# Talking-heads attention with a squared-ReLU feed-forward: PSUM as three two-bank tiles and two single banks, merged copies, and the first batch's feed-forward in three token groups

## The chip, the cores and the metric

The kernel runs on one core of one Trainium2 chip. The metric is the device time of one execution in microseconds, and a kernel's time is the median of its runs. A ratio is the mean time of one kernel's fast runs over that of the other kernel's fast runs of the same rounds on the same chip, with a 95% interval, so it is not quite the ratio of the medians that are quoted beside it. A difference of over 2% counts as faster or slower.

Engines are named as in the profile: PE multiplies matrices, DVE and ACT copy and compute, POOL computes `d` and `h` here (360 times 641 ns and 128 times 931 ns in the kernel before), PEld is PE's weight load.

## The reference

Eight batches of attention with 12 heads, 448 tokens and 64 dimensions per head. Scores are mixed across heads before and after the softmax, and the result goes through a two-layer feed-forward.

```python
scores = scale * np.matmul(q, k.transpose(0, 1, 3, 2))
scores = np.einsum('bhij,hg->bgij', scores, w_pre)      # mix over heads
scores = scores - np.max(scores, axis=-1, keepdims=True)
attn = np.exp(scores)
attn = attn / (np.sum(attn, axis=-1, keepdims=True) + 1e-09)
attn = np.einsum('bhij,hg->bgij', attn, w_post)         # mix over heads again
attn_out = np.matmul(attn, v)
# ... [cut: heads put side by side: x is 3584 x 768]
h = np.maximum(x @ w_in, 0.0)                            # w_in is 768 x 2048
out = h * h @ w_out                                      # w_out is 2048 x 768
```

## The kernel before

The work on one batch is cut into 45 tiles of up to 10 query rows (all 12 heads of them). The kernel goes through the tiles two at a time; such a pair is called a **step** here, and a batch has 22.5 steps. In a step PE makes:

- `s_ps`: scores of a head pair for a coming block; ACT or DVE copies them to the buffer S, and a DMA gathers S into tiles G with heads and rows side by side;
- `m_ps`: the first mixing of two tiles; ACT takes the exponential, POOL normalises into `d`;
- `at_ps`: the second mixing of the two tiles mixed two steps earlier; DVE casts the result into `at`.

Between these there are four kinds of larger work: `tr_ps` (transposes of the next batch's k and q, six units per batch), `ot_ps` (attention times v, two units after each of three parts of a batch), and the feed-forward of the batch before, `h_ps` (first layer, 16 units) and `o_ps` (second layer, 7 tiles in two halves each). The feed-forward is a filler: it is dealt out evenly over the steps.

```python
psp = ctx.enter_context(tc.tile_pool(name="psp", bufs=8, space=bass.MemoryType.PSUM))
def bank(name, dtype=F32):                     # all eight banks are one pool
    return psp.tile([P, 512 if dtype == F32 else 1024], dtype, name=name, tag="ps")

def score_burst(b, blk, pairs):
    # ... [cut]
    for p in pairs:
        for hh in range(2):
            # ... [cut]
            ps = bank("s_ps")
            nc.tensor.matmul(ps[:, 0:S], ...)
            got.append((2 * p + hh, ps))
    for h, ps in got:                          # one copy per head, one bank each
        if h % 2 == 0 or (b == 0 and h in (3, 9)):
            nc.scalar.copy(out=sb[:, h, :], in_=ps[:, 0:S])
        else:
            nc.vector.tensor_copy(out=sb[:, h, :], in_=ps[:, 0:S])

def unmix(pair):
    us = [bank("at_ps") for _ in range(2)]     # two banks, two casts
    # ... [cut]

def fill(ns):                                  # the filler, with a debt
    owed[0] += ns
    while filler and owed[0] > 0:
        w, f = filler.pop(0)
        f()
        owed[0] -= w
    # ... [cut]
# ... [cut: most of the loop over the steps]
    fill(share)
    for w, f in now:                           # transposes and ot_ps units of this step
        f()
        owed[0] -= w                           # their time is taken from the filler
```

The softmax here doesn't subtract the row's maximum and nothing guards it: scores larger than these inputs give would overflow.

## Time and profile before

| | before |
|---|---|
| median of 3 runs | 639.2 us (638.43 to 642.54) |
| span of the profiled run, mean granted clock | 637.8 us, 0.942 |
| busy: PE, DVE, ACT, POOL | 580.7, 414.9, 403.5, 405.7 us |

The page cuts the span into 40 slices of 15.9 us. Of the kernel before, these are the rows of PE's busy share and of its granted clock, both in tenths (9 is 90% or more):

```profile
PE   4558678699999999999999999999999999999897
PEclk9675686799999999999999999999999999999899
```

The first eight slices, up to some 125 us, are a different regime: PE is busy 0.4 to 0.8 of the time and its clock, from the second slice on, is at 0.5 to 0.8. (The 9 of the first slice is not a clock that was granted: the trace's clock records begin with the first change, at 14.1 us here, and the row counts the time before it as full. Sixteen `tr_ps` matmuls took 0.96 us at 5.5 us, and 0.56 us at 38.7 us, where the recorded clock is full.) After that PE is over 90% busy at full clock (1.00 from 124 to 580 us) until the last batch's feed-forward. The stretches view (start and end in us, length, busy time and instruction count of PE, PEld, DVE, ACT and POOL, then granted clock, share of the DMA engines and GB/s) of the kernel before:

```profile
60.00:100.00 40.00, 28.27 (x344) 11.85 (x338) 27.16 (x73) 26.66 (x84) 23.65 (x36) 0.71 0.72 126
...
191.60:226.00 34.40, 33.62 (x420) 17.28 (x421) 26.28 (x65) 27.32 (x79) 31.39 (x44) 1.00 0.68 110
297.70:327.30 29.60, 29.41 (x421) 16.79 (x414) 24.05 (x60) 18.73 (x60) 13.93 (x23) 1.00 0.68 140
```

In the first row nothing is saturated. In the second (a batch's first-layer half) PE has 33.62 of 34.40 us and POOL 31.39; in the third (a second-layer half) PE has 29.41 of 29.60.

The waits view (who waited for whom; us in total, times, the longest) of the kernel before, 0 to 119 us, shows that score copies wait for the gathers that still read the buffer they are to overwrite:

```profile
ACT S L296 <- DMA G<-S: 24.0, 5, 7.5
...
DVE S L298 <- DMA G<-S: 13.7, 4, 4.9
```

The groups of copies that the change merges, from the page of the kernel before (line, engine, operation, output<-input, shapes, count | busy us, mean ns of one | idle time just before, what ended most of it):

```profile
L351 DVE CAST at<-at_ps 112x480 bf16<-112x480 f32 x352 | 221.3, 669 | 41.7 <-PE at_ps L344 41.1
...
L296 ACT CAST S<-s_ps 128x448 bf16<-128x448 f32 x200 | 105.9, 550 | 55.7 <-PE s_ps L291 27.4
...
L298 DVE CAST S<-s_ps 128x448 bf16<-128x448 f32 x184 | 110.6, 607 | 16.3 <-DMA G<-S 13.7
```

PE's own waits of the kernel before, from the start of step 48 to that of step 179 (181.8 to 580.3 us, almost six batches):

```profile
PE o_ps L254 <- POOL h L232: 2.1, 3, 0.9
PE s_ps L291 <- ACT e_sb L319: 1.0, 5, 0.2
PE at_ps L344 <- ACT xt L192: 0.9, 2, 0.5
...
```

And a piece of PE's timeline of the kernel before (start us, duration us, what; the count is of single matmuls). Three transpose units and two `ot_ps` units, each with a bank of its own, follow each other without a gap:

```profile
178.51 0.58 PE L162 MATMUL tr_ps<-ident,kst 112*64 112x112 bf16 x16
178.93 0.56 PE L162 MATMUL tr_ps<-ident,qst 112*64 112x112 bf16 x16
179.32 0.56 PE L162 MATMUL tr_ps<-ident,kst 112*64 112x112 bf16 x16
179.71 1.61 PE L181 MATMUL ot_ps<-at,v 112*64 112x138 bf16 x48
181.25 0.39 PE L344 MATMUL at_ps<-post,d 60*128 60x60 bf16 x16
```

### The profile page before, as it was taken

To read this page: it belongs to the slowest core of one execution; us is meant where nothing else is said; L and a number is where in the kernel's file an instruction comes from. 1 tells how busy PE (TensorE), PEld (TensorE's weight loads), DVE (VectorE), ACT (ScalarE), POOL (GpSimd) and SP (SyncE) were. 2 spreads that over 40 slices of the span, in tenths; PEclk is the share of its full clock that TensorE was granted. 3 is DMA by queue.
4 is the path that set the end of the run, shared out by engine and by line. 5 is a ranking of instruction groups with operands and counts; after the bars stand their busy time and mean duration, and the time that the engine had idled before them with its cause. 6 is when DMAs were issued, how large, how long until landed. Compare 5 with 4: busy or idle time off the path is not lost.

```text
span 637.8 us, 19148 instructions
## 1 busy us (share of the span) xinstructions
PE 580.7 (91%) x7338; PEld 313.8 (49%) x7338; DVE 414.9 (65%) x1050; ACT 403.5 (63%) x1196; POOL 405.7 (64%) x583
## 2 busy tenths in 40 slices
PE   4558678699999999999999999999999999999897
PEld 3125234345555456455555455545555555555454
DVE  3366666566777767777787677776787677755101
ACT  3656567477467865887578756886587757862330
POOL 6343558699448963888468943897387746873350
PEclk9675686799999999999999999999999999999899
DMA  9884869997655785578646885488543655432002
GB/s 135 141 170 85 153 108 197 197 187 111 139 113 89 127 150 121 92 110 136 140 103 106 135 157 104 87 135 135 126 94 74 110 128 103 81 61 64 25 7 81
DMA packets 90880, 73.61 MB, mean 115 GB/s; under 512 B 6308, under 2 KB 87716, under 8 KB 90788
## 3 DMA queue, kind: packets, MB, share of 16 engines
q1 hardware_dynamic: 51842, 49.57, 34.6%
q0 software_dynamic: 38816, 22.81, 27.8%
q8 instruction: 57, 0.93, 0.6%
q14 instruction: 35, 0.29, 0.1%
q10 hardware_dynamic: 130, 0.01, 0.0%
HBM read 45.63 MB, written 11.01 MB: 89 GB/s over the span
## 4 chain that ended last, share of the span: by engine, by line
PE 67%; POOL 11%; ACT 8%; DMA 5%; DVE 4%; SPq 2%; issue 2%; ACTq 0%; POOLq 0%; DVEq 0%
PE o_ps L254 23%; PE h_ps L227 18%; PE m_ps L316 9%; PE at_ps L344 6%; PE ot_ps L181 5%; POOL d L323 5%; DMA G<-S 4%; POOL h L232 4%; PE s_ps L291 4%; ACT xt L192 3%; ACT e_sb L319 3%; PE tr_ps L162 2%; SPq L310 2%; DVE at L351 2%; ACT S L296 2%
## 5 line engine op out<-in xcount | busy, mean ns | idle before, releaser
L323 POOL TENSOR_SCALAR d<-e_sb,rc 128x448 bf16<-128x448 f32 x360 | 226.7, 641 | 178.0 <-DVE rc L321 175.3
L351 DVE CAST at<-at_ps 112x480 bf16<-112x480 f32 x352 | 221.3, 669 | 41.7 <-PE at_ps L344 41.1
L319 ACT ACTIVATE e_sb<-m_ps 128x448 f32<-128x448 f32 x360 | 195.4, 556 | 59.2 <-PE m_ps L316 51.0
L227 PE MATMUL h_ps<-xt,w 128*128 128x448 bf16 x768 | 167.0, 357 | 0.2 <-ACT e_sb L319 0.2
L254 PE MATMUL o_ps<-w,h 128*128 128x384 bf16 (+1 forms) x1024 | 162.4, 327 | 2.1 <-POOL h L232 2.1
L296 ACT CAST S<-s_ps 128x448 bf16<-128x448 f32 x200 | 105.9, 550 | 55.7 <-PE s_ps L291 27.4
L232 POOL TENSOR_TENSOR h<-hr 128x448 bf16<-128x448 f32 x128 | 118.4, 931 | 26.9 <-ACT hr L231 26.5
L298 DVE CAST S<-s_ps 128x448 bf16<-128x448 f32 x184 | 110.6, 607 | 16.3 <-DMA G<-S 13.7
L316 PE MATMUL m_ps<-G,pre 120*128 120x448 bf16 x360 | 108.0, 374 | 14.4 <-DMA G<-S 6.2
L254 PEld LDWEIGHTS <-h 128*128 128x128 bf16 (+1 forms) x1024 | 85.4, 100 | 71.2 <-issue 16.8
L321 DVE RECIPROCAL rc<-sm 128x1 f32<-128x1 f32 x360 | 55.8, 159 | 99.1 <-ACT e_sb L319 96.2
L227 PEld LDWEIGHTS <-w 128*128 128x128 bf16 x768 | 71.4, 98 | 76.8 <-issue 17.0
L231 ACT ACTIVATE hr<-h_ps 128x448 f32<-128x448 f32 x128 | 70.4, 550 | 44.1 <-PE h_ps L227 33.7
L344 PEld LDWEIGHTS <-d 60*128 60x128 bf16 x2880 | 54.7, 96 | 75.4 <-issue 54.6
L344 PE MATMUL at_ps<-post,d 60*128 60x60 bf16 x2880 | 76.6, 192 | 8.7 <-ACT S L296 6.0
L291 PE MATMUL s_ps<-kT,qT 64*128 64x448 bf16 x384 | 78.2, 370 | 3.1 <-ACT e_sb L319 1.3
L319 ACT ACTIVATION_READ_ACCUMULATOR e_sb<-m_ps 128x1 f32 x360 | 77.9, 216 | 0.0
L192 ACT ACTIVATE xt<-ot_ps,bvec 128x160 bf16<-128x160 f32 (+3 forms) x144 | 42.8, 392 | 43.5 <-PE ot_ps L181 30.8
L316 PEld LDWEIGHTS <-pre 120*128 120x128 bf16 x360 | 29.6, 99 | 54.3 <-issue 25.1
L181 PE MATMUL ot_ps<-at,v 112*64 112x160 bf16 (+4 forms) x1152 | 46.6, 242 | 9.6 <-ACT S L296 5.9
L261 DVE COPY osb<-o_ps 128x384 f32<-128x384 f32 x48 | 26.4, 551 | 39.0 <-PE o_ps L254 37.9
L181 PEld LDWEIGHTS <-v 112*64 112x64 bf16 x1152 | 43.1, 118 | 14.8 <-issue 12.0
(35 smaller groups left out, 189.7 us busy)
## 6 DMA issues: line engine op xcount, KB each, us to landing
G<-S SPq DMA_DIRECT2D x352, 105.0 KB
kst<-in_k_dram POOLq DMA_DIRECT2D x24, 224.0 KB, 5.9
qst<-in_q_dram POOLq DMA_DIRECT2D x24, 224.0 KB, 5.5
v<-in_v_dram POOLq DMA_DIRECT2D x24, 224.0 KB, 6.6
w<-in_moe_w_in_dram POOLq DMA_DIRECT2D x8, 384.0 KB, 6.5
w<-in_moe_w_out_dram POOLq DMA_DIRECT2D x8, 384.0 KB, 9.6
out_dram<-osb SPq DMA_DIRECT2D x8, 336.0 KB
out_dram<-osb SPq DMA_DIRECT2D x8, 288.0 KB
```

Of the source, the lines that this page charges most:

```text
L181: nc.tensor.matmul(ps[64 * hh:64 * hh + 64, TW * y + c0:TW * y + 2 + n], lhsT=vs[b][0:PR, g, r, :], rhs=at[0:PR, r, g, c0:2 + n], start=(y ...
L227: nc.tensor.matmul(ps[:, 0:S], lhsT=w1[ft // 4][:, c2, ft % 4 * 128:ft % 4 * 128 + 128], rhs=xts[b][:, c2, :], start=(c2 == 0), stop=(c2 = ...
L232: nc.gpsimd.tensor_tensor(out=h2[:, :], in0=hr[:, :], in1=hr[:, :], op=ALU.mult)
L254: nc.tensor.matmul(dst, lhsT=h2ts[(b, ft)][:, mt * 128:mt * 128 + ROWS[mt]], rhs=w2[ft // 4][:, ft % 4, n2 * 384:(n2 + 1) * 384], start=(f ...
L291: nc.tensor.matmul(ps[:, 0:S], lhsT=qTs[b][rs, p, BLK_START[blk]:BLK_START[blk] + P], rhs=kTs[b][rs, p, :], start=True, stop=True)
L296: nc.scalar.copy(out=sb[:, h, :], in_=ps[:, 0:S])
L298: nc.vector.tensor_copy(out=sb[:, h, :], in_=ps[:, 0:S])
L316: nc.tensor.matmul(ps[:, 0:S], lhsT=pre[0:n, :], rhs=Gs.pop(s)[0:n, :], start=True, stop=True)
L319: nc.scalar.activation(out=e[:, :], in_=ps[:, 0:S], func=ACT.Exp, scale=SCALE, accum_out=sm[:, 0:1])
L323: nc.gpsimd.tensor_scalar(out=d[:, 0:S], in0=e[:, :], scalar1=rc[:, 0:1], scalar2=-1.0 / S, op0=ALU.mult, op1=ALU.add)
L344: nc.tensor.matmul(us[y][:, c:c + HR], lhsT=d[rows, PR * r:PR * r + P], rhs=post[rows, :], start=True, stop=True)
L351: nc.vector.tensor_copy(out=dst[:, :, :, y, :], in_=src)
```

## The change

The intent has two parts. The first: two tiles' results lie side by side in a two-bank PSUM tile, so one copy evacuates both, and is to take less time than two (after: 908 ns against 2 x 550 on ACT, 1079 against 2 x 607 on DVE). The second: PE idles in the first 120 us, so two thirds of batch 0's first-layer work is moved there: as soon as a third of batch 0's tokens has its attention, the first layer is run on these tokens alone. For that the weights load earlier, and scores follow the gathers later; the transposes of batch 1 move from steps 6 and 8 to steps 15 and 17.

```diff
-    psp = ctx.enter_context(tc.tile_pool(name="psp", bufs=8, space=bass.MemoryType.PSUM))
+    psd = ctx.enter_context(tc.tile_pool(name="psd", bufs=3, space=bass.MemoryType.PSUM))
+    psp = ctx.enter_context(tc.tile_pool(name="psp", bufs=2, space=bass.MemoryType.PSUM))
+    def two_banks(name):
+        return psd.tile([P, 2, 512], F32, name=name, tag="psd")
 
-    def ffn1_unit(b, ft):
+    def ffn1_unit(b, ft, c0=0, c1=S):          # on tokens c0 to c1
...
+        if n < S and ft % 2:
+            nc.vector.tensor_scalar_max(out=hr[:, 0:n], in0=ps[:, 0:n], scalar1=0.0)
...
-    def score_burst(b, blk, pairs):
+    def score_pair(b, blk, p):
+        ps = two_banks("s_ps")
+        for hh in range(2):
+            nc.tensor.matmul(ps[:, hh, 0:S], ...)
+        copy = nc.vector.tensor_copy if p % 2 else nc.scalar.copy
+        copy(out=Sb[(b, blk)][:, 2 * p:2 * p + 2, :], in_=ps[:, :, 0:S])
...
-    def mix(s):
-        ps = bank("m_ps")
+    def mix(pair):
+        ps = two_banks("m_ps")
...
     def unmix(pair):
-        us = [bank("at_ps") for _ in range(2)]
+        u = two_banks("at_ps")                 # and one cast of both banks
...
-            load_v(0, x)
+            at_load(4 + x, load_v, 0, x)
-            at_load(3 * x - 6 if x > 1 else -1, load_qk, 1, x)
+            at_load(8 + 2 * x, load_qk, 1, x)
-            at_load(9 + 5 * x if x else 8, load_w1, x)
-            at_load(52 + 2 * x, load_w2, x)
+            at_load(-1 if x < 4 else x - 4, load_w1, x)
+            at_load(20 + 2 * x, load_w2, x)
...
-                score_burst(*blocks[issued[0] // NPAIR], [issued[0] % NPAIR])
+                score_pair(*blocks[issued[0] // NPAIR], issued[0] % NPAIR)   # one step later than before
...
+            if ds <= EARLY[2]:                 # EARLY = [10, 18, 25]
+                rest = 1 + min(x for x in EARLY if x >= ds) - ds
...
+                        if b1 == 0:
+                            c = (IQ * ends[part], min(IQ * ends[part + 1], S))
+                            at_step(ds + 1, (0, lambda c=c: filler.extend(ffn1_units(0, *c))))
```

(Lines of three dots mark cuts; a few lines inside the functions shown are left out too; the comments are added here.) `h_ps`, `o_ps`, `tr_ps` and `ot_ps` still call `bank`, so they now share the two single banks.

More of the change, by code (lines that the diff above doesn't have):

```diff
@@ L36 @@
 SCALE = 1.0 / 8.0
-TURN = {0: (6, 8), 1: (7, 8 + LAG), B: (2, 8 + LAG)}
+FIRST_TURN = (15, 17)
+TURN = {0: FIRST_TURN, 1: (7, 8 + LAG), B: (2, 8 + LAG)}
+EARLY = [10, 18, 25]
 ROWS = [128, 128, 128, 64]
@@ L222, in load_w2 @@
                             in_=moe_w_out[n * x:n * x + n, :].rearrange("(c p) m -> p c m", p=P))
-    def ffn1_unit(b, ft):
+    def ffn1_unit(b, ft, c0=0, c1=S):
         ps = bank("h_ps")
+        n = c1 - c0
         for c2 in range(NPAIR):
-            nc.tensor.matmul(ps[:, 0:S], lhsT=w1[ft // 4][:, c2, ft % 4 * 128:ft % 4 * 128 + 128], rhs=xts[b][:, c2, :],
-                             start=(c2 == 0), stop=(c2 == NPAIR - 1))
-        h2 = ffnp.tile([P, S], BF16, name="h2", tag="h2", bufs=FT + 1)
+            nc.tensor.matmul(ps[:, 0:n], lhsT=w1[ft // 4][:, c2, ft % 4 * 128:ft % 4 * 128 + 128],
+                             rhs=xts[b][:, c2, c0:c1], start=(c2 == 0), stop=(c2 == NPAIR - 1))
+        if (b, ft) not in h2ts:
+            h2ts[(b, ft)] = ffnp.tile([P, S], BF16, name="h2", tag="h2", bufs=FT + 1)
         hr = ffnp.tile([P, S], F32, name="hr", tag="hr", bufs=2)
-        nc.scalar.activation(out=hr[:, :], in_=ps[:, 0:S], func=ACT.Relu)
-        nc.gpsimd.tensor_tensor(out=h2[:, :], in0=hr[:, :], in1=hr[:, :], op=ALU.mult)
-        h2ts[(b, ft)] = h2
+        if n < S and ft % 2:
+            nc.vector.tensor_scalar_max(out=hr[:, 0:n], in0=ps[:, 0:n], scalar1=0.0)
+        else:
+            nc.scalar.activation(out=hr[:, 0:n], in_=ps[:, 0:n], func=ACT.Relu)
+        nc.gpsimd.tensor_tensor(out=h2ts[(b, ft)][:, c0:c1], in0=hr[:, 0:n], in1=hr[:, 0:n], op=ALU.mult)
     o_open, osbs = {}, {}
@@ L270, in ffn2_unit, with ffn1_units, ffn2_units @@
                                   in_=osb[64 * n2:64 * n2 + 64, :])
-    def ffn_units(b):
-        u = [(1140, lambda ft=ft: ffn1_unit(b, ft)) for ft in range(FT)]
+    def ffn1_units(b, c0=0, c1=S):
+        return [(int(2.54 * (c1 - c0)), lambda ft=ft: ffn1_unit(b, ft, c0, c1)) for ft in range(FT)]
+    def ffn2_units(b):
+        u = []
         for mt, nt in [(mt, nt) for mt in range(3) for nt in range(2)] + [(3, 0)]:
@@ L279 @@
     Sb, Gs, dsb = {}, {}, {}
-    def score_burst(b, blk, pairs):
+    def score_pair(b, blk, p):
         if (b, blk) not in Sb:
             Sb[(b, blk)] = work.tile([P, H, S], BF16, name="S", tag="S", bufs=2)
-        sb = Sb[(b, blk)]
-        got = []
-        for p in pairs:
-            for hh in range(2):
-                rs = slice(64 * hh, 64 * hh + 64)
-                ps = bank("s_ps")
-                nc.tensor.matmul(ps[:, 0:S], lhsT=qTs[b][rs, p, BLK_START[blk]:BLK_START[blk] + P],
-                                 rhs=kTs[b][rs, p, :], start=True, stop=True)
-                got.append((2 * p + hh, ps))
-        for h, ps in got:
-            if h % 2 == 0 or (b == 0 and h in (3, 9)):
-                nc.scalar.copy(out=sb[:, h, :], in_=ps[:, 0:S])
-            else:
-                nc.vector.tensor_copy(out=sb[:, h, :], in_=ps[:, 0:S])
+        ps = two_banks("s_ps")
+        for hh in range(2):
+            rs = slice(64 * hh, 64 * hh + 64)
+            nc.tensor.matmul(ps[:, hh, 0:S], lhsT=qTs[b][rs, p, BLK_START[blk]:BLK_START[blk] + P],
+                             rhs=kTs[b][rs, p, :], start=True, stop=True)
+        copy = nc.vector.tensor_copy if p % 2 else nc.scalar.copy
+        copy(out=Sb[(b, blk)][:, 2 * p:2 * p + 2, :], in_=ps[:, :, 0:S])
     def rows_of(t):
@@ L311, in gather @@
         Gs[s] = g
-    def mix(s):
-        n = rows_of(s[1])
-        ps = bank("m_ps")
-        nc.tensor.matmul(ps[:, 0:S], lhsT=pre[0:n, :], rhs=Gs.pop(s)[0:n, :], start=True, stop=True)
-        e = work.tile([P, S], F32, name="e_sb", tag="E", bufs=3)
-        sm = work.tile([P, 1], F32, name="sm", tag="sm", bufs=4)
-        nc.scalar.activation(out=e[:, :], in_=ps[:, 0:S], func=ACT.Exp, scale=SCALE, accum_out=sm[:, 0:1])
-        rc = work.tile([P, 1], F32, name="rc", tag="rc", bufs=4)
-        nc.vector.reciprocal(out=rc[:, :], in_=sm[:, :])
-        d = dts[(NT * s[0] + s[1]) % ND]
-        nc.gpsimd.tensor_scalar(out=d[:, 0:S], in0=e[:, :], scalar1=rc[:, 0:1], scalar2=-1.0 / S,
-                                op0=ALU.mult, op1=ALU.add)
-        dsb[s] = d
+    def mix(pair):
+        ps = two_banks("m_ps")
+        for x, s in enumerate(pair):
+            n = rows_of(s[1])
+            nc.tensor.matmul(ps[:, x, 0:S], lhsT=pre[0:n, :], rhs=Gs.pop(s)[0:n, :], start=True, stop=True)
+        for x, s in enumerate(pair):
+            e = work.tile([P, S], F32, name="e_sb", tag="E", bufs=3)
+            sm = work.tile([P, 1], F32, name="sm", tag="sm", bufs=4)
+            nc.scalar.activation(out=e[:, :], in_=ps[:, x, 0:S], func=ACT.Exp, scale=SCALE, accum_out=sm[:, 0:1])
+            rc = work.tile([P, 1], F32, name="rc", tag="rc", bufs=4)
+            nc.vector.reciprocal(out=rc[:, :], in_=sm[:, :])
+            d = dts[(NT * s[0] + s[1]) % ND]
+            nc.gpsimd.tensor_scalar(out=d[:, 0:S], in0=e[:, :], scalar1=rc[:, 0:1], scalar2=-1.0 / S,
+                                    op0=ALU.mult, op1=ALU.add)
+            dsb[s] = d
     def place_of(s):
@@ L343, in unmix @@
                     c = 4 * HR * x + HR * r
-                    nc.tensor.matmul(us[y][:, c:c + HR], lhsT=d[rows, PR * r:PR * r + P], rhs=post[rows, :],
+                    nc.tensor.matmul(u[:, y, c:c + HR], lhsT=d[rows, PR * r:PR * r + P], rhs=post[rows, :],
                                      start=True, stop=True)
         (at, c), (at2, c2) = places
-        for y in range(2):
-            src = us[y][0:PR, 0:8 * HR].rearrange("p (x m i) -> p m x i", x=2, i=HQ)
-            if at is at2:
-                dst = at[0:PR, :, :, c:c + 2 * IQ].rearrange("p r g (x z i) -> p (r g) x z i", z=2, i=HQ)
-                nc.vector.tensor_copy(out=dst[:, :, :, y, :], in_=src)
-            else:
-                for x, (a, p) in enumerate(places):
-                    dst = a[0:PR, :, :, p + HQ * y:p + HQ * y + HQ].rearrange("p r g i -> p (r g) i")
-                    nc.vector.tensor_copy(out=dst, in_=src[:, :, x, :])
+        src = u[0:PR, :, 0:8 * HR].rearrange("p y (x m i) -> p m x y i", x=2, i=HQ)
+        if at is at2:
+            dst = at[0:PR, :, :, c:c + 2 * IQ].rearrange("p r g (x y i) -> p (r g) x y i", y=2, i=HQ)
+            nc.vector.tensor_copy(out=dst, in_=src)
+        else:
+            for x, (a, p) in enumerate(places):
+                dst = a[0:PR, :, :, p:p + IQ].rearrange("p r g (y i) -> p (r g) y i", i=HQ)
+                nc.vector.tensor_copy(out=dst, in_=src[:, :, x, :, :])
     filler = []
@@ L381 @@
             if x > 0:
-                score_burst(0, 0, [2 * x - 2, 2 * x - 1])
-        for x in range(2):
-            score_burst(0, 1, [3 * x, 3 * x + 1, 3 * x + 2])
-        for x in range(AHEAD):
-            gather(steps[x])
+                score_pair(0, 0, 2 * x - 2)
+                score_pair(0, 0, 2 * x - 1)
         nc.gpsimd.dma_start(out=wpost_bf[:, :], in_=w_post[0:H, 0:H])
@@ L391, in at_load @@
             loads.setdefault(i, []).append(lambda: f(*args))
+        for x in range(8):
+            at_load(-1 if x < 4 else x - 4, load_w1, x)
+            at_load(20 + 2 * x, load_w2, x)
         for x in range(3):
-            load_v(0, x)
+            at_load(4 + x, load_v, 0, x)
             at_load(48 + x, load_v, 1, x)
         for x in range(6):
-            at_load(3 * x - 6 if x > 1 else -1, load_qk, 1, x)
+            at_load(8 + 2 * x, load_qk, 1, x)
             at_load([45, 46, 47, 53, 55, 57][x], load_qk, 2, x)
-        for x in range(8):
-            at_load(9 + 5 * x if x else 8, load_w1, x)
-            at_load(52 + 2 * x, load_w2, x)
         for b in range(1, B):
@@ L410, with scores_for @@
         starts = [NT * b + TPB * blk for b, blk in blocks] + [len(steps)]
-        issued = [2 * NPAIR]
-        def scores_up_to(tile):
+        issued, gathered = [NPAIR], [0]
+        def scores_for(ds):
+            tile = 2 * ds + AHEAD + 2
             blk = sum(tile >= x for x in starts) - 1
@@ L416, in scores_up_to, with gathers_for @@
                 return
-            size = starts[blk + 1] - starts[blk]
-            want = NPAIR * (blk + 1) + -(-NPAIR * (tile - starts[blk]) // size)
-            while issued[0] < want:
-                score_burst(*blocks[issued[0] // NPAIR], [issued[0] % NPAIR])
-                issued[0] += 1
+            if blk == 3:
+                want = NPAIR * 4 + 2 * max(0, ds - FIRST_TURN[1])
+            else:
+                into, size = tile - starts[blk] - 2, starts[blk + 1] - starts[blk] - 2
+                want = NPAIR * (blk + 1) + -(-NPAIR * into // size)
+            while issued[0] < min(want, NPAIR * (blk + 2)):
+                score_pair(*blocks[issued[0] // NPAIR], issued[0] % NPAIR)
+                issued[0] += 1
+        def gathers_for(ds):
+            while gathered[0] < min(2 * ds + AHEAD + 2, len(steps)):
+                b, t = steps[gathered[0]]
+                if issued[0] < NPAIR * (4 * b + t // TPB + 1):
+                    break
+                gather(steps[gathered[0]])
+                gathered[0] += 1
+        gathers_for(-1)
         for f in loads.get(-1, []):
@@ L438 @@
             rest = ((NT + 1) // 2 + LAG - ds) % (NT / 2) + 1
+            if ds <= EARLY[2]:
+                rest = 1 + min(x for x in EARLY if x >= ds) - ds
             share = sum(w for w, _ in filler) / rest / 2 if now2 else 1e9
             now = timed.pop(ds, [])
-            for s in now2:
-                mix(s)
+            if now2:
+                mix(now2)
             fill(share)
@@ L451 @@
                     if t1 + 1 in ends:
-                        for u in av_units(b1, ends.index(t1 + 1) - 1):
+                        part = ends.index(t1 + 1) - 1
+                        for u in av_units(b1, part):
                             at_step(ds + 1, u)
+                        if b1 == 0:
+                            c = (IQ * ends[part], min(IQ * ends[part + 1], S))
+                            at_step(ds + 1, (0, lambda c=c: filler.extend(ffn1_units(0, *c))))
                     if t1 == NT - 1:
-                        at_step(ds + 1, (0, lambda b1=b1: filler.extend(ffn_units(b1))))
-            for i in (2 * ds + AHEAD, 2 * ds + AHEAD + 1):
-                if i < len(steps):
-                    gather(steps[i])
-            scores_up_to(2 * ds + AHEAD + 2)
+                        if b1 > 0:
+                            at_step(ds + 1, (0, lambda b1=b1: filler.extend(ffn1_units(b1))))
+                        at_step(ds + 1, (0, lambda b1=b1: filler.extend(ffn2_units(b1))))
+            scores_for(ds)
+            gathers_for(ds)
             if ds + 1 < nd + LAG:
```

## The prediction

> **What bounds the kernel now.** The table of stretches shows three regimes.
>
> 1. 0 to 119 us: nothing is saturated. PE is busy about 0.7 of the time at a granted clock of 0.50 to 0.84. The waits view of this stretch charges ACT and DVE 37.7 us to score copies (S) waiting for gathers (DMA G<-S) that still read the buffer to be overwritten; the PE timeline shows gaps at 42.4-49.4, 74.9-81.1 and 113-118 us.
> 2. 119 to 593 us, batches of 67 to 72 us. In the first-layer half (h_ps) POOL is the limit (31.4 of 34.4 us busy in 191.6-226; d takes 641 ns, h 931). In the second-layer half (o_ps) PE is (29.4 of 29.6 us in 297.7-327.3).
> 3. 593 to 638 us: the last batch's feed-forward, PE alone.
>
> **What the change does.**
>
> *Moves.* Two of batch 0's three token groups of ffn1 (320 of 448 tokens, 13.5 of about 19 us of PE work) go into regime 1, where PE is idle. Batch 1's period loses them, and its POOL-bound half shrinks (h on 128 tokens: an estimated 0.35 us; weight loads come earlier). I expect 119-191.6 (72.6 us) to become about 61: gain 12.
>
> *Slack.* Scores follow gathers one step later, so the S buffer wait has about two steps instead of one. Against it: all 3.1 MB of second-layer weights now load inside batch 0, where DMA already moves 107 to 214 GB/s; at about 200 GB/s the bytes up to the point now reached at 119 us need about 90. I expect about 100: gain 19. PE work should also lift the clock: [...] this trace agrees, 0.5-0.84 before 119 us and 1.00 after.
>
> *Merged copies.* 384 S copies (ACT 550, DVE 607 ns) become 192 of an estimated 920 ns (ACT; its 896-wide copy takes 906) and 1070 ns (DVE); 352 casts of 669 ns become 176 of an estimated 1170. DVE falls by about 30 us, ACT by about 20. [...] DVE and ACT are busy 0.65 to 0.8 here: almost nothing gained.
>
> *PSUM.* h, o, transposes and attention-value tiles now share two banks instead of eight. Where an o_ps is open, three transposes and two ot_ps units pass through one bank: each transpose then waits for a 0.6 us DVE copy (about 1.05 us after its last matmul), the second ot_ps for three xt activations (about 1.5 us). The instruction order shows about five such waits in odd batches, fewer in even ones; with the tighter three two-bank tiles I estimate 2 to 6 us lost per batch, partly hidden where POOL limits: about 20 us in all.
>
> **Sum:** 639 - 12 - 19 + 20 = 628; I take 627 us, range 606 to 645. Chances: faster 0.47, same 0.45, slower 0.08.
>
> **Right or wrong.** h_ps matmuls of 160 columns appear before 100 us, with clock above 0.85 in 60-100 us; batch 1's second-layer work ends near 160 us; S<-G waits at most half of 37.7 us; the waits view shows new PE waits (tr_ps, ot_ps) on DVE kT/qT copies and ACT xt; DVE busy about 385, ACT about 385 us; later batch periods 69 to 74 us.
>
> **What would make it wrong.** Loads starving the gathers, so batch 0 gets no shorter (650); or bank waits absorbed by slack or the scheduler, so steady batches stay at 69 us (605).

The 0.35 us for `h` on 128 tokens was the estimate; after's trace has 0.396.

## More of the kernel before

Counted from the program, an average step takes 7.7 banks: 6.1 for `m_ps`, `at_ps` and `s_ps` (360, 360 and 384 in 180 steps), and 1.6 for `h_ps`, `o_ps`, `tr_ps` and `ot_ps` (128, 56, 48 and 48). This counts how often a bank is taken, not how many are held at once.

## The result, and the profile after

| | before | after |
|---|---|---|
| median of 4 runs, same rounds | 640.22 us | 683.93 us (681.78 to 684.3) |
| ratio | | 1.0674, interval 1.0629 to 1.0718: slower |
| span of the profiled run, granted clock | 637.8 us, 0.942 | 681.9 us, 0.977 |
| busy: PE, DVE, ACT, POOL | 580.7, 414.9, 403.5, 405.7 | 584.2, 408.4, 393.7, 409.5 |

PE has nearly the same busy time, and 44.1 us more span. The same rows of the page after, in slices of 17.0 us:

```profile
PE   4468777778799998988999987989999988999897
PEclk9999899999789999999989998989999999999999
```

The clock row of the first eight slices looks high, but its first three slices must not be read so: the first clock record of this trace is a change to full at 57.4 us. Before it the clock was not full, as the durations of the score matmuls show (shortest, median and longest in ns, first and last start in us; in before they took 528 to 557 ns between 21 and 38 us, at a recorded clock of 0.50, and 347 to 359 between 38 and 45 us, at 1.00):

```profile
L301 PE MATMUL s_ps<-kT,qT x42: 527/552/578, 12.1 to 52.7; 64*128 64x448 bf16 x42
L301 PE MATMUL s_ps<-kT,qT x14: 346/350/360, 57.9 to 79.7; 64*128 64x448 bf16 x14
```

So the mean granted clocks of the table don't compare either. With half the clock up to the first record they would be, by an estimate from these numbers, 0.931 before and 0.935 after. From 57.4 us on the clock is higher than before, as intended. But PE's row has 8s and 7s all through the middle, where it had 9s, and the clock has two low slices of its own, at 170 to 204 us.

To see where the 44.1 us lie, the trace is cut at steps, not at microseconds: the start of a step is the start of its first `m_ps` matmul, rounded to 0.1 us. Steps 0 to 26 are batch 0 and a little more, 26 to 48 roughly batch 1, 48 to 179 all later batches, and the rest is the last batch's feed-forward. (The third column is an experiment that is explained below.)

| us | before | after | after's order of work with before's banks |
|---|---|---|---|
| up to step 0 | 20.9 | 24.6 | 23.3 |
| steps 0 to 26 | 83.3 | 85.7 | 80.2 |
| steps 26 to 48 | 77.6 | 76.5 | 66.0 |
| steps 48 to 179 | 398.5 | 439.0 | 400.3 |
| rest | 57.5 | 56.1 | 57.5 |
| sum (span) | 637.8 | 681.9 | 627.3 |

So 40.5 of the 44.1 us are lost after step 48, where the change moved no feed-forward at all, and the two stages that were to become shorter did not: +2.4 and -1.1 us, after a first step that came 3.7 us later.

PE's waits after, over the same steps (186.8 to 625.8 us):

```profile
PE ot_ps L187 <- ACT xt L198: 8.2, 8, 1.1
PE s_ps L301 <- ACT e_sb L327: 7.5, 13, 0.8
PE at_ps L352 <- DVE at L358: 6.9, 12, 0.6
PE m_ps L323 <- DVE at L358: 5.6, 8, 0.9
PE tr_ps L168 <- DVE kT L170: 2.3, 4, 1.0
PE tr_ps L168 <- DVE qT L170: 1.8, 3, 0.7
PE ot_ps L187 <- DVE kT L170: 1.0, 4, 0.3
...
```

Every one of these lines is PE waiting for a reader of a PSUM bank to give it back. Two families are seen. `tr_ps` and `ot_ps` wait for readers of the two single banks. `s_ps`, `at_ps` and `m_ps` wait for readers of the three two-bank tiles: a score tile waits until both exponentials of an `m_ps` tile have been taken, an `m_ps` tile until the long cast of an `at_ps` tile is over. Summed over every gap of PE above 0.1 us between these steps, PE's idle time went from 6.0 us (before) to 37.1 us: `ot_ps` and `tr_ps` 14.7, `m_ps`, `s_ps` and `at_ps` 21.9, `o_ps` 0.5.

The stretches view over just these steps (columns as above), first of before:

```profile
181.80:580.30 398.50, 391.87 (x5173) 213.26 (x5172) 295.36 (x741) 283.78 (x856) 277.92 (x397) 1.00 0.61 112
```

and then of after:

```profile
186.80:625.80 439.00, 401.61 (x5154) 220.03 (x5154) 284.38 (x540) 279.63 (x788) 276.38 (x395) 0.98 0.55 101
```

The length grew by 40.5 us. PE's busy time grew by 9.74 us for nearly the same work (5173 and 5154 matmuls), and its idle time, 6.63 us before and 37.39 after, by 30.76. So three quarters of the loss show as waits, and a quarter as records of matmuls that cover more time.

The same burst of transposes and `ot_ps` units as shown before, in PE's timeline after (in brackets: PE idle before it, and who ended that):

```profile
176.93 0.56 PE L168 MATMUL tr_ps<-ident,kst 112*64 112x112 bf16 x16
178.22 0.58 PE L168 MATMUL tr_ps<-ident,qst 112*64 112x112 bf16 x16 [0.72 <-DVE kT L170]
179.52 0.58 PE L168 MATMUL tr_ps<-ident,kst 112*64 112x112 bf16 x16 [0.71 <-DVE qT L170]
180.82 1.59 PE L187 MATMUL ot_ps<-at,v 112*64 112x138 bf16 x24 [0.71 <-DVE kT L170]
183.41 1.59 PE L187 MATMUL ot_ps<-at,v 112*64 112x138 bf16 x24 [1.00 <-ACT xt L198]
184.93 0.58 PE L352 MATMUL at_ps<-post,d 60*128 60x60 bf16 x16
```

At that point an `o_ps` tile is open and holds one of the two single banks, so five units go one after the other through the other bank. Before, the time from the first transpose to the next `at_ps` was 181.25 - 178.51 = 2.74 us; now it is 184.93 - 176.93 = 8.00 us. The four bracketed waits make 3.14 of the 5.26 us. Most of the rest is in the matmuls: 24 `ot_ps` matmuls took 1.59 us each time, while before 48 of them took 1.61. The stretches view after shows a lower clock:

```profile
60.00:100.00 40.00, 30.48 (x510) 21.67 (x510) 28.80 (x62) 24.14 (x72) 28.97 (x53) 0.96 0.79 151
177.00:187.00 10.00, 6.35 (x119) 4.83 (x116) 3.45 (x6) 2.70 (x7) 0.95 (x2) 0.66 0.53 113
187.00:193.00 6.00, 5.58 (x56) 2.46 (x54) 4.28 (x8) 3.11 (x9) 2.53 (x4) 0.50 0.39 70
```

PE was busy 6.35 of the 10 us of the burst, and the clock went down to one half; by the trace's clock records it stayed there for 13.7 us from 180.3 us on, while PE was busy again (5.58 of 6 us). Three more spells at half clock follow, at 344.1, 415.8 and 449.9 us, of 3.4 us each. Before had none from 124 us to step 179. In the 3.4 us (the length of the three short spells) before each of the four spells PE was busy for only 1.77, 1.91, 1.71 and 1.68 us, with gaps of 0.4 to 1.0 us. Two of them (180.3 and 415.8) follow a burst of transposes; the other two follow waits of `m_ps`, `s_ps` and `at_ps` for the two-bank tiles, with no transpose among them. Such gaps need not bring a spell: the burst at 256.6 us has the same two waits as the one at 411.8 (0.99 and 0.71 us, PE busy 1.70 of 3.40 us), and the clock stayed full (1.00). The first row shows the other side: from 60 to 100 us the clock was 0.96 instead of 0.71.

The merged copies after, from the page:

```profile
L358 DVE CAST at<-at_ps 112x960 bf16<-112x960 f32 x176 | 202.5, 1151 | 56.8 <-PE at_ps L352 56.0
...
L304 DVE CAST S<-s_ps 128x896 bf16<-128x896 f32 x96 | 103.4, 1079 | 9.0 <-DMA G<-S 4.5
L304 ACT CAST S<-s_ps 128x896 bf16<-128x896 f32 x96 | 87.0, 908 | 33.0 <-PE s_ps L301 28.0
```

One merged copy costs less than two single ones by their means: 1151 against 2 x 669, 1079 against 2 x 607, 908 against 2 x 550 ns, so 187, 135 and 192 ns less. DVE's busy time fell by 6.5 us all the same, not by the 30 us of the prediction. The durations of all DVE records (count times mean of every group) sum to 475.1 us before and 440.1 after, which is 35.0 less, with 7.4 us of new relus in it. But the busy time counts a moment once even where the records of two instructions overlap: 60.2 us of before's sum were such overlap (475.1 - 414.9), and 31.7 of after's. Most of what the merging took away had been hidden behind the neighbour already.

The waits for gathers after, 0 to 119 us:

```profile
PE m_ps L323 <- DMA G<-S: 7.6, 1, 7.6
...
ACT S L304 <- DMA G<-S: 4.8, 1, 4.8
...
DVE S L304 <- DMA G<-S: 4.5, 1, 4.5
```

The copies' waits fell from 37.7 to 9.3 us, but one wait of 7.6 us of PE itself for a gather is new, and the stage is not shorter.

### The profile page after: what moved, and what is told of

Same layout as the page of the kernel before. It is cut to its first block, busy times and chain, and to the rows that moved or that the text cites. A ratio compares the mean times of both kernels' runs of the same rounds, so it can differ in the third digit from the quotient of the medians.

```text
span 681.9 us, 19218 instructions
## 1 busy us (share of the span) xinstructions
PE 584.2 (86%) x7530; PEld 331.1 (49%) x7530; DVE 408.4 (60%) x802; ACT 393.7 (58%) x1100; POOL 409.5 (60%) x615
## 3 DMA queue, kind: packets, MB, share of 16 engines
q1 hardware_dynamic: 51842, 49.57, 33.6%
## 4 chain that ended last, share of the span: by engine, by line
PE 62%; ACT 12%; DVE 7%; POOL 7%; DMA 5%; issue 5%; SPq 2%; ACTq 0%; DVEq 0%; POOLq 0%
PE o_ps L264 22%; PE h_ps L234 16%; PE m_ps L323 8%; ACT e_sb L327 6%; PE ot_ps L187 6%; PE at_ps L352 5%; DMA G<-S 4%; PE s_ps L301 3%; ACT xt L198 3%; POOL d L331 3%; DVE at L358 3%; POOL h L243 2%; PE tr_ps L168 2%; ACT S L304 2%; SPq L316 2%
## 5 line engine op out<-in xcount | busy, mean ns | idle before, releaser
L358 DVE CAST at<-at_ps 112x960 bf16<-112x960 f32 x176 | 202.5, 1151 | 56.8 <-PE at_ps L352 56.0
L234 PE MATMUL h_ps<-xt,w 128*128 128x448 bf16 (+2 forms) x960 | 171.0, 320 | 7.5 <-ACT hr L242 3.7
L243 POOL TENSOR_TENSOR h<-hr 128x448 bf16<-128x448 f32 (+2 forms) x160 | 123.6, 780 | 26.9 <-ACT hr L242 25.7
L323 PE MATMUL m_ps<-G,pre 120*128 120x448 bf16 x360 | 104.4, 373 | 20.6 <-DMA G<-S 8.6
L234 PEld LDWEIGHTS <-w 128*128 128x128 bf16 x960 | 83.2, 99 | 78.4 <-issue 22.2
L304 DVE CAST S<-s_ps 128x896 bf16<-128x896 f32 x96 | 103.4, 1079 | 9.0 <-DMA G<-S 4.5
L304 ACT CAST S<-s_ps 128x896 bf16<-128x896 f32 x96 | 87.0, 908 | 33.0 <-PE s_ps L301 28.0
L242 ACT ACTIVATE hr<-h_ps 128x448 f32<-128x448 f32 (+2 forms) x136 | 68.4, 503 | 48.9 <-PE h_ps L234 37.7
L352 PE MATMUL at_ps<-post,d 60*128 60x60 bf16 x2880 | 73.4, 192 | 14.7 <-DVE at L358 9.8
L301 PE MATMUL s_ps<-kT,qT 64*128 64x448 bf16 x384 | 68.9, 380 | 17.1 <-ACT e_sb L327 13.0
L327 ACT ACTIVATION_READ_ACCUMULATOR e_sb<-m_ps 128x1 f32 x360 | 73.5, 204 | 0.0
L323 PEld LDWEIGHTS <-pre 120*128 120x128 bf16 x360 | 30.5, 99 | 53.6 <-issue 28.9
```

Source lines behind the costliest of these rows:

```text
L234: nc.tensor.matmul(ps[:, 0:n], lhsT=w1[ft // 4][:, c2, ft % 4 * 128:ft % 4 * 128 + 128], rhs=xts[b][:, c2, c0:c1], start=(c2 == 0), stop=( ...
L242: nc.scalar.activation(out=hr[:, 0:n], in_=ps[:, 0:n], func=ACT.Relu)
L243: nc.gpsimd.tensor_tensor(out=h2ts[(b, ft)][:, c0:c1], in0=hr[:, 0:n], in1=hr[:, 0:n], op=ALU.mult)
L301: nc.tensor.matmul(ps[:, hh, 0:S], lhsT=qTs[b][rs, p, BLK_START[blk]:BLK_START[blk] + P], rhs=kTs[b][rs, p, :], start=True, stop=True)
L304: copy(out=Sb[(b, blk)][:, 2 * p:2 * p + 2, :], in_=ps[:, :, 0:S])
L323: nc.tensor.matmul(ps[:, x, 0:S], lhsT=pre[0:n, :], rhs=Gs.pop(s)[0:n, :], start=True, stop=True)
```

## The experiments

Twelve kernels were run; all gave correct results. Each has 4 runs (3 timed rounds and the profiled run); the kernel before had 637.31, 639.77 and 638.35 us as median.

The theories at the outset were these. *The banks* (theory P in the expectations): dividing PSUM costs the time, either by the bursts of `tr_ps` and `ot_ps` through two single banks (P1), or because the six other banks are too few for `s_ps`, `m_ps` and `at_ps`, or because a merged copy holds two banks longer (P2). *The order* (theory O): the earlier feed-forward, the earlier loads and the later scores of batch 0 cost the time, by starving gathers or by crowding DVE, ACT and POOL.

### 1. Each half of the change alone

`ffn_only` is the kernel after with before's PSUM: one pool of eight, single-bank tiles and copies. `psum_only` is the kernel before with after's PSUM: 3 two-bank tiles, 2 single banks, merged copies.

```diff
 # ffn_only, against the kernel after
-    psd = ctx.enter_context(tc.tile_pool(name="psd", bufs=3, ...))
-    psp = ctx.enter_context(tc.tile_pool(name="psp", bufs=2, ...))
+    psp = ctx.enter_context(tc.tile_pool(name="psp", bufs=8, ...))
 # score_burst, mix and unmix as in the kernel before
```

> The changed kernel's order of work (three token groups of the first feed-forward, earlier weight loads, later scores) with the eight single banks and the one-bank copies of the kernel before. Theory P: about 13 us of batch 1 are saved and nothing is lost later, 620 to 632 us. Theory O: 660 us or more.

> The kernel before with only the PSUM side of the change: three two-bank tiles for s, m and at, two single banks for the rest, one copy per tile pair; loads, order of scores and feed-forward as before. Theory P (the banks and copies cost the time): batches after the first stay about 6 us longer than before each, total 670 to 685 us. Theory O (the new order of work costs the time): 635 to 645 us.

| | median us | ratio to before | steps 0-26 | 26-48 | 48-179 |
|---|---|---|---|---|---|
| before | 637.31 | | 83.3 | 77.6 | 398.5 |
| ffn_only | 628.08 | 0.9848 (0.9798 to 0.9897) | 80.2 | 66.0 | 400.3 |
| psum_only | 668.48 | 1.0492 (1.0427 to 1.0556) | 77.4 | 82.6 | 429.6 |
| after (from the result above) | 683.93 | 1.0674 (1.0629 to 1.0718) | 85.7 | 76.5 | 439.0 |

The order of work alone takes 1.5% off the time (too little for the 2% rule, which leaves it unclear); the banks alone make it 4.9% slower, at 668.48 us just under the 670 to 685 that was expected. The theory that the order costs the time fails, as far as the order stands alone. The two do not add up, though: -9 and +31 would give 22, and the change lost 44. With `ffn_only`, PE hardly waits between steps 48 and 179; its largest waits there are these:

```profile
PE s_ps L300 <- ACT e_sb L331: 2.0, 11, 0.2
PE o_ps L260 <- POOL h L239: 1.3, 2, 0.7
...
```

### 2. Is it the division, the pairing, or the merged copy?

`split62` is the kernel before with one thing changed: `s_ps`, `m_ps` and `at_ps` take single banks from a pool of six, the rest from a pool of two. Copies and order are before's. `split53` gives five and three. `psum_2copies` is `psum_only` with two one-bank copies for each two-bank tile.

```diff
 # split62 (split53: 3 and 5), against the kernel before
-    psp = ctx.enter_context(tc.tile_pool(name="psp", bufs=8, space=bass.MemoryType.PSUM))
+    psp = ctx.enter_context(tc.tile_pool(name="psp", bufs=2, space=bass.MemoryType.PSUM))
+    psa = ctx.enter_context(tc.tile_pool(name="psa", bufs=6, space=bass.MemoryType.PSUM))
...
-                ps = bank("s_ps")
+                ps = bank_a("s_ps")              # the same for m_ps and at_ps
```

```diff
 # psum_2copies, against psum_only (the same for the at casts)
-        copy = nc.vector.tensor_copy if p % 2 else nc.scalar.copy
-        copy(out=Sb[(b, blk)][:, 2 * p:2 * p + 2, :], in_=ps[:, :, 0:S])
+        for hh, h in ((0, 2 * p), (1, 2 * p + 1)):
+            if h % 2 == 0 or (b == 0 and h in (3, 9)):
+                nc.scalar.copy(out=Sb[(b, blk)][:, h, :], in_=ps[:, hh, 0:S])
+            else:
+                nc.vector.tensor_copy(out=Sb[(b, blk)][:, h, :], in_=ps[:, hh, 0:S])
```

> The kernel before with its eight single banks divided: six for s, m and at, two for h, o, transposes and attention-value; copies of one bank each as before. Theory P1 (the two shared banks are too few: bursts of three transposes and two ot_ps units wait for their own copies): 655 to 670 us, with PE waits of tr_ps on DVE copies and ot_ps on ACT xt. Theory P2 (the long copies of tile pairs cost the time): within 1% of before, 635 to 646 us.

> As split62 (662 us against 637), but five banks for s, m and at, and three for the rest. Theory P1 (how many banks the bursts share sets the loss): the third bank takes the tr_ps and ot_ps waits away, unless five banks are now too few for the others; 637 to 650 us. If it stays at 655 or more, the count of shared banks is not what matters.

> As psum_only (668 us), but each two-bank tile is read by two one-bank copies as in the kernel before. Between split62 (662) and psum_only (668) lie the pairing of banks and the merging of copies. If the long copies cost: 662 us or less. If merging them helps: 672 us or more. If neither: 665 to 670 us.

| before's order of work, with | median us | ratio to before |
|---|---|---|
| six and two single banks (split62) | 662.39 | 1.0375 (1.0311 to 1.0438) |
| five and three single banks (split53) | 671.76 | 1.0504 (1.0463 to 1.0546) |
| three pairs and two singles, two copies (psum_2copies) | 664.83 | 1.0408 (1.0368 to 1.0449) |
| three pairs and two singles, one copy (psum_only) | 668.48 | 1.0492 (1.0427 to 1.0556) |

Dividing the pool six to two, and nothing else, costs 25 of psum_only's 31 us. Pairing and merging add little: the intervals of the six-and-two, the paired and the merged kernel touch or overlap. The 664.83 us of psum_2copies lie between two of its expected bands. So no gain from merging the copies is seen, and with what the runs resolve it may have cost a few microseconds.

The result of split53 was a miss for the theory of the bursts. PE's waits of split62, from step 48 to step 179:

```profile
PE ot_ps L185 <- ACT xt L196: 8.2, 8, 1.1
PE at_ps L348 <- ACT S L300: 4.1, 13, 0.4
PE tr_ps L166 <- DVE kT L168: 2.4, 4, 0.8
PE tr_ps L166 <- DVE qT L168: 2.1, 4, 0.7
...
```

and of split53, over the same steps:

```profile
PE m_ps L320 <- DVE at L355: 9.2, 33, 0.4
PE s_ps L295 <- DVE at L355: 3.0, 8, 0.4
PE at_ps L348 <- ACT e_sb L323: 2.8, 8, 0.4
...
PE tr_ps L166 <- DVE kT L168: 0.8, 2, 0.4
...
```

The third bank did what was expected of it: PE's idle time before `tr_ps` and `ot_ps` fell from 14.1 to 0.8 us. But the bank came from the other pool, and PE's idle time before `m_ps`, `s_ps` and `at_ps` rose from 7.0 to 22.4 us. The 5+3 split moved the shortage instead of removing it.

The idle time does not hold the whole loss, though. Split53 took 431.0 us for these steps, split62 422.2, before 398.5; PE's busy time for the same 5173 matmuls was 406.6, 399.1 and 391.9 us, in split53 at a granted clock of 1.00 throughout. So the records can cover more time without any change of the clock, here 14.7 us; what is in it, short waits perhaps, the traces do not show.

### 3. How many banks does the kernel need?

`banks7` and `banks6` are the kernel before with a shared pool of seven and of six.

```diff
-    psp = ctx.enter_context(tc.tile_pool(name="psp", bufs=8, space=bass.MemoryType.PSUM))
+    psp = ctx.enter_context(tc.tile_pool(name="psp", bufs=6, space=bass.MemoryType.PSUM))   # banks7: 7
```

> The kernel before with seven shared single banks instead of eight, nothing else. Theory D (dividing the banks costs: idle ones of one kind can't serve the other): seven shared banks lose less than half of what split62 loses with eight divided ones, 637 to 650 us. Theory N (the kernel needs all eight, however they are handed out): 655 us or more.

> As banks7 with six shared banks. Theory D: at or below split62's 662 us. Theory N: 675 us or more.

With seven the kernel took 644.18 us (ratio 1.0083, 1.004 to 1.0125), with six 662.91 (1.0389, 1.034 to 1.0438). With seven, the expectation of theory D (division costs) is met and that of theory N (all eight are needed) is not; with six, the time is 0.9 us above D's bound. So eight banks split six to two (662.39) are as slow as six banks that everybody may use, and slower than seven. PE's largest waits with six, over the same steps:

```profile
PE m_ps L316 <- ACT xt L192: 7.6, 19, 0.5
PE at_ps L344 <- ACT e_sb L319: 2.3, 5, 0.5
...
```

The `xt` activations read the `ot_ps` banks, and it is `m_ps` that waits for them: in a shared pool a shortage hits whichever work comes next, in many short waits (19 of at most 0.5 us). Here too idle time is only part of the loss: of 22.4 us in these steps 10.1 are idle time, and PE's busy time rose by the other 12.4 (the mean granted clock of the whole profiled run was 0.938, of before's 0.942). In the divided pools the same shortage makes 8 waits of up to 1.1 us before `ot_ps`. These runs show that it is the division that costs, since seven shared banks lose less than eight divided ones: the kernel before was near the edge with eight banks (one less already costs 0.8%, six cost 3.9%). The reason is inferred from the waits: a division takes away the lending between the kinds of work. While a burst of `tr_ps` and `ot_ps` passes, it could borrow; in between, `m_ps`, `s_ps` and `at_ps` could use all but one or two.

### 4. The bursts spread over steps

`spread` is the kernel after, with one transpose unit per step where there were three in one, and the two `ot_ps` units of a part in two steps.

```diff
 # against the kernel after
-                            at_step(ds + TURN.get(b, TURN[B])[x // 3], u)
+                            t0 = TURN.get(b, TURN[B])[x // 3]
+                            at_step(ds + (t0 if b == 0 else (t0 if x < 3 else 7) + x % 3), u)
...
-                        for u in av_units(b1, part):
-                            at_step(ds + 1, u)
+                        for x, u in enumerate(av_units(b1, part)):
+                            at_step(ds + 1 + x, u)
```

(The first transposes of batch 1 also begin at step 4 instead of 7, and the filler is extended one step later.)

> The changed kernel with its bursts taken apart: one transpose unit per step instead of three, and the two attention-value units of a part in two steps. Theory P1: the single-bank waits go, 684 falls to 655 to 668 us. Theory P2: stays above 678 us.

It took 662.05 us (1.0393 to before, 1.0331 to 1.0455), 21.9 less than after: 9.4 us came in steps 26 to 48 (76.5 to 67.1) and 12.9 in steps 48 to 179 (439.0 to 426.1). So spreading the bursts gave back two fifths of the 56 us that the division costs with this order (after against ffn_only), and in batch 1 nearly all of it (67.1 us, ffn_only 66.0). The other changes of place in `spread` were not tested apart. Most of the rest is not in bursts: in steps 48 to 179 PE still idles 11.0 us before `m_ps` and 6.5 before `s_ps`, beside 6.4 before `ot_ps`.

### 5. The token groups alone

`ffn_nogroups` and `after_nogroups` are `ffn_only` and after without the token groups: the whole first layer of batch 0 runs in batch 1's period, as before, but loads and scores keep the new order.

```diff
-            if ds <= EARLY[2]:
-                rest = 1 + min(x for x in EARLY if x >= ds) - ds
...
-                        if b1 == 0:
-                            c = (IQ * ends[part], min(IQ * ends[part + 1], S))
-                            at_step(ds + 1, (0, lambda c=c: filler.extend(ffn1_units(0, *c))))
...
-                        if b1 > 0:
-                            at_step(ds + 1, (0, lambda b1=b1: filler.extend(ffn1_units(b1))))
+                        at_step(ds + 1, (0, lambda b1=b1: filler.extend(ffn1_units(b1))))
```

> ffn_only (628 us) without the three token groups: eight single banks, the changed loads and order of scores alone. If the groups are the gain of ffn_only: 637 to 645 us. If the loads and the later scores are: 625 to 632 us.

> The changed kernel without the three token groups: the first layer of batch 0 runs whole after its attention, as in the kernel before; loads, order of scores and banks as in the changed kernel. With ffn_nogroups, ffn_only (628) and the changed kernel (684) this makes a table of two by two. If groups and banks are independent, the groups are worth about 12 us here too: about 695 us. If the small units lose their gain on two banks (each unit of 160 tokens is about 0.5 us of PE work, its copy and release take about 1 us): 680 to 688 us.

Put with the runs above, this gives a two-by-three table (medians, us):

| | before's order | new loads and scores | and token groups |
|---|---|---|---|
| eight shared banks | 637.3 to 639.8 | 634.5 | 628.1 |
| three pairs and two singles | 668.5 | 680.2 | 683.9 |

With shared banks each step of the order helps: 3 to 6 us for loads and scores, 4 to 6 for the groups (the smaller or larger number according to whether medians or the ratios are compared; the kernel before itself differed by 2.5 us, and the intervals of the ratios with and without groups, from 0.9868 and up to 0.9897, overlap a little). The 634.5 us of ffn_nogroups lie between its two expected bands, so neither part is the whole gain. By stages, the groups took 9.2 us from steps 26 to 48 (75.2 to 66.0) and added 4.2 to steps 0 to 26 (76.0 to 80.2). With divided banks the loads and scores cost 8 to 12 us, and the groups do not help any more (680.2 and 683.9 us, with intervals of the ratios that overlap), as its expectation had it for small units that lose their gain. (In after's trace such a unit of 160 columns takes PE 0.59 us, and its relu is over 0.92 us after the unit began: 61.95 to 62.87 us.) For the groups the profile points to a reason: 48 short units instead of 16, all through the two single banks, each with its relu to wait for, beside transposes and `ot_ps` units. From step 0 to step 48 PE waits 7.1 us before `h_ps` for the relus in after, and in ffn_only, for other readers, 2.1 us. Why loads and scores cost more there is not settled (5.8 of them lie in steps 48 to 179, 435.4 against 429.6, so it is not the loads, which are over by then; the later and denser scores remain).

### 6. Two attempts at a better version

`ffn_loads` is `ffn_only` with the first-layer weights loaded later, to let the first gathers start earlier; `ffn_weights` counts a whole first-layer unit as 1388 instead of 1137 ns when the filler is dealt out, to spread the work that POOL limits.

```diff
 # ffn_loads
-            at_load(-1 if x < 4 else x - 4, load_w1, x)
-            at_load(20 + 2 * x, load_w2, x)
+            at_load(2 * x, load_w1, x)
+            at_load(36 + 2 * x, load_w2, x)
 # ffn_weights
-        return [(int(2.54 * (c1 - c0)), ...
+        return [(int((3.1 if c1 - c0 == S else 2.54) * (c1 - c0)), ...
```

> ffn_only (628 us) with its weight loads spread: one first-layer load per step from step 0 instead of eight by step 2, second-layer loads from step 18 instead of 10. If the loads hold back the gathers of batch 0: the first mix starts about 2 us earlier (near 21 us instead of 23.3), the 8 us wait of PE for a gather before it shrinks, total 618 to 624 us. If they don't: 626 to 630 us.

> ffn_only with one number changed: a whole first-layer unit counts 3.1 ns per column instead of 2.54 when the feed-forward is spread over the steps, so that the half of a batch in which POOL limits gets more steps. If the POOL limit of that half is real, later batches shorten by 1 to 3 us each: 612 to 624 us. If not: 626 to 634 us.

Neither gained anything. `ffn_loads` took 635.49 us (0.9944, 0.9898 to 0.9991), 7 more than `ffn_only` and above both expected bands: step 0 did come earlier (21.2 instead of 23.3 us), but the waits of score copies for gathers rose from 11.5 to 21.3 us and step 26 came at 107.5 instead of 103.5 us. `ffn_weights` took 629.88 us (0.9867, 0.9827 to 0.9907), no different from `ffn_only`: the outcome that was expected if POOL's limit in that half is not real.

The best version found is `ffn_only`, at 628.08 us: 1.5% below before and 8% below after. By the 2% rule that is neither "same" nor "faster" but unclear, since its interval, 0.9798 to 0.9897, contains 0.98.

## Why the prediction was wrong

It said 627 us with a range of 606 to 645; the kernel took 683.93. Its sum was 639 - 12 - 19 + 20. Point by point:

1. **The PSUM term (+20) was mis-sized; this is the step that failed, with 36 of the 57 us by which the prediction was off.** (The other 21 are the terms -12 and -19: together the order gained 9 us with before's banks, not 31. See 2 and 3.) "I estimate 2 to 6 us lost per batch, partly hidden where POOL limits: about 20 us in all." The mechanism was right, and the waits it named are there: `tr_ps` on kT and qT copies, `ot_ps` on xt activations, about 1 us each. The size was 31 us alone (psum_only against before, 668.5 - 637.3), and 56 us with the new order (after against ffn_only, 683.9 - 628.1). Two things were left out. First, only the bursts were counted. `m_ps`, `s_ps` and `at_ps` on six banks were waved off as "tighter", and they make 21.9 of PE's 37.1 us of idle time in steps 48 to 179. Second, the clock was counted as a gain only: after stretches with gaps it went down to one half for 13.7 us, and for 3.4 us three times later. Between steps 48 and 179 PE's idle time rose by 30.8 us and its busy time by 9.7, together the 40.5 us lost there. The half-clock time in these steps is about 17 us (7 of the long spell and 3 x 3.4), an estimated 8 us of lost work if PE was busy through it, so the clock could explain most of the 9.7. But split53's busy time grew by 14.7 us with the clock full throughout (1.00), so this is not shown, and no run took the clock's part away by itself. "Partly hidden where POOL limits" cannot have been much: before, PE had 33.6 of 34.4 us there too, and ffn_weights, which gave that half more steps, gained nothing.

2. **The slack term (-19) started from a wrong point.** "I expect about 100" for "the point now reached at 119 us" took the first `h_ps` as the end of batch 0. The steps show otherwise: step 26 starts at 104.2 us in before; the first `h_ps` comes 4 to 5 steps later because the filler has a debt to work off (six transposes of 430, six `ot_ps` units of 800 and 100 ns: 7.5 us). So batch 0 was already nearly where the prediction wanted it. At step 31, which before reaches at 121.5 us, after is at 125.8 and ffn_only at 118.3. That is -3; ffn_nogroups, without the groups' work in it, is there at 112.9, -9 at best, not -19. The mechanism was right in part: the copies' waits for gathers fell from 37.7 to 9.3 us, below the half that was predicted. Those were waits of DVE and ACT, and little came of them; presumably these two were not the limit.

3. **Moving the groups (-12) was right in kind, and undone by the banks.** From step 31 to step 48, ffn_only took 51.2 us where before took 60.3, so -9; after took 61.0. The 13.5 us of PE work really went into idle time with eight banks, at a cost of 4.2 us in batch 0. On two single banks nothing was left of it. "Batch 1's second-layer work ends near 160 us" failed: the last `o_ps` matmul of that period ended at 193.5 us in after, at 187.3 in before and at 174.1 in ffn_only.

4. **The merged copies were right in time and wrong in busy time.** "Almost nothing gained" holds: 665 us with two copies, 668 with one (psum_2copies and psum_only). The single durations were close (908, 1079 and 1151 ns against 920, 1070 and 1170), the busy times not: DVE 408.4 instead of 385, ACT 393.7 instead of 385. A mean duration times a count is more than busy time where instructions overlap (475.1 against 414.9 us on DVE before). DVE was busy for 0.65 of before's span, and no gain from merging is seen; psum_2copies is even the faster of the two, by 4 us, within overlapping intervals.

5. **The clock in 60 to 100 us was right**: above 0.85 was predicted, 0.96 was measured (0.71 before), and 1.00 with ffn_only. The groups' work has a part in it: without the groups it was 0.80 (after_nogroups) and 0.83 (ffn_nogroups). It did not shorten batch 0: after took 85.7 us from step 0 to step 26 and ffn_only 80.2, against 83.3 before. (Up to 57.4 us after's clock was at one half, by the 527 to 578 ns of its `s_ps` matmuls, while ffn_only had 17 us of full clock by then; whether this makes part of the difference was not tested.) PE was not the limit from 60 to 100 us, with 30.5 of 40 us busy. What is, stays open.

6. **The later periods** were predicted at 69 to 74 us. From one batch's first `h_ps` to the next they were, from batch 1's (at 194.6 us) on, 75.0, 80.2, 77.7, 76.5, 72.7 and 63.9 us (before: 68.9, 70.6, 68.3, 71.5, 66.9, 61.4). Four of the six lie above the predicted span, so the check that the prediction itself had set failed with it.

That the reasoning had listed "bank waits absorbed by slack" as a risk on the fast side, and no risk on the slow side except starving loads, shows the blind spot: bank waits were allowed to be smaller than estimated, never larger.

What stays open: how much of the growth of PE's busy time is the clock; why the new loads and scores cost 8 to 12 us with divided banks and gain 3 to 6 with shared ones; and what limits batch 0 at 76 us or more from step 0 to step 26.

## What to carry to other kernels

A pool of PSUM banks that several kinds of work share can lend its idle banks to whoever has a burst. Before you divide it, count the banks per step (7.7 here, with eight banks) and run the kernel with one and with two banks less: here seven already cost 0.8%, and six and two cost as much as six alone. With PE busy for 0.91 of before's span, waits for banks went to the time (30.8 of the 40.5 us lost after step 48), and four stretches of them were followed by half the clock for 3.4 to 13.7 us. Check what the first clock record of a trace covers before you compare clocks (after's first 57.4 us count as full, and were not). And judge a move of work by steps that mean the same in both kernels; the first appearance of a filler is not the end of a stage.
